# A new order table and new transfer times in the planner of a cluster-attention and expert-attention kernel

## The chip, the cores and the metric

The kernel runs on one core of one Trainium2 chip. The metric is the device time of one execution in microseconds (us), as the median of several runs of the same program. The kernel before has three runs, 741.66, 745.32 and 745.89 us, so its median is 745.32 us. One further execution was taken with the hardware profiler.

## What is computed

The reference is two attentions, one after the other (B = 4, S = 768, eight heads of 64, then four experts of 64 on 512 columns):

```python
q_assign = argmax(q_n @ c_n)          # 16 clusters a head; the same for the keys
scores = where(q_assign == k_assign, scale * q @ k.T, -1e9)
x = softmax(scores) @ v               # batch x sequence x 512
logits = x @ w_gate                   # top 2 of 4 experts, softmax over the two
for e in range(E):                    # causal attention of each expert
    ye = softmax(causal(scale * (x @ wq[e]) @ (x @ wk[e]).T)) @ (x @ wv[e]) @ wo[e]
    out += gate_e * ye
```

## The kernel before

The work is cut into 24 visits, numbered n: sixteen pairs of heads (n = 0 to 15) and eight pairs of experts (n = 16 to 23). For a pair of heads, `attention_operands` loads k, q and v, turns k and q on TensorE (L627), finds the clusters, and puts the operands for the scores into one of three sets of tiles, `tk` and `tq`, by DMA: the high and low parts of k and q, and the one-hot cluster rows (`place_rows`, four transfers for q and four for k). For a pair of experts `moe_operands` makes k and q from x (L871), and `moe_values` makes v and the gates: a chain of very small DVE instructions (L940 to L952), one exponential, five more small ones (L958 to L962), then a transpose on TensorE (L967).

`core(n)` is the same for both. Row products (L1085) give the scores of 128 queries against all keys; DVE takes their maximum (L1095); the maxima are turned (L1107) and go by DMA into `tq` as one more row, so that the second product, of scores laid out key block by key block (L1159, L1160), comes out with the maximum subtracted. ACT takes the exponential of each key block into a tile p (L1165), in the expert stage POOL clears what lies above the diagonal (L1170), and the products with v (L1203) sum p times v into `av`. They run as a **visit**: for most pairs of heads one visit takes all six key blocks of a half of the queries, 24 instructions of 128x384 in the profile. Sums over the p tiles (L480 on POOL or L481 on DVE, by the table) give the denominators, which go through a product with ones (L1223), a DMA to DRAM (`sd`), back (`r`), a reciprocal, to DRAM (`rd`) and back spread out (`rb`).

Nothing is left to a scheduler on the chip. Each piece of work is an `op` (L278) with an engine, a duration in the planner's eyes, what it comes after and which buffers it uses; some have a second engine that may take them (`alt`). `ORDER` (L37 to L216) is a table of the numbers of these ops, one list for each engine, which says in what order each engine runs them and, for ops with a choice, on which engine. `Plan.run` walks the table, gives buffers their slots by the times it works out, and emits the code. All DMAs are issued by SP, in the order of its list. The times that the planner assumes for a transfer are a pair (issue, move), such as `(0.45, 1.65)` for a load of q or k, plus `REACH` from the end of issue to the start of the move (L259). They do nothing on the chip by themselves: they decide which order a search finds and which slot a buffer gets. The waits on the chip come from what each instruction reads and writes. A transfer also waits for the landing of the one eight places ahead of it, since eight semaphores are shared in turn.

Two things in the planner matter below. An op that is marked `port` isn't placed beside work on POOL. And `needs` (L289) can give a dependence with a lead: the op may start before that piece is done. Before the change a visit of products with v waits, in the planner, for all its p tiles, and frees all of them at its end.

## Time and profile before

| | us |
|---|---|
| median of three runs | 745.32 |
| profiled execution, own time | 740.65 |
| its span, first to last instruction | 738.4 |
| PE busy / DVE busy / ACT busy / POOL busy | 707.2 / 552.6 / 369.5 / 335.0 |

The own time of the profiled execution is 2.25 us more than its span, and 4.67 us less than the median of the runs. PE is TensorE's matmuls, PEld its weight loads, DVE VectorE, ACT ScalarE, POOL GpSimd and SP the engine that issues the DMAs. A matmul of 384 columns counts as 0.34 us busy, but the next one starts 0.17 to 0.18 us later: they are pipelined, so a busy PE isn't PE at its peak, while an idle one is a real wait. An entry such as `[2.88 <-DMA tk<-xh]` in a list in order of time is the idle time ahead of the instruction and what ended it.

### The profile page before, as it was taken

The numbers are of one execution on the slowest core, as the hardware profiler recorded it, in microseconds if no ns is written. First come the engines' busy times: TensorE is split into PE (matmuls) and PEld (weight loads), VectorE is DVE, ScalarE is ACT, GpSimd is POOL, SyncE is SP. The second block draws the span as 40 slices with busy tenths as digits, with TensorE's granted clock in tenths as the row PEclk, the third lists the DMA queues.
The fourth block names the chain that finished last, engine by engine and source line by source line (L and its number), as shares of the span: only waits on it lengthen the run. The fifth ranks groups of instructions, "written<-read, shape, count | busy, mean of one in ns | idle before, by whom it ended". The sixth has DMA issues, their size and how long they took to land.

```text
span 738.4 us, 13669 instructions
## 1 busy us (share of the span) xinstructions
PE 707.2 (96%) x4607; PEld 531.0 (72%) x4607; DVE 552.6 (75%) x1249; ACT 369.5 (50%) x912; POOL 335.0 (45%) x267
## 2 busy tenths in 40 slices
PE   6889999999999999999999999989999999999997
PEld 5656757667676676676666689758877987987676
DVE  7978878878888788788778767783497389658733
ACT  4455647556565465466466542444353345434541
POOL 5034357664763864865786442153422223200530
PEclk9999999999999999999999999999999999999999
DMA  7796546485766686664776563525454545354223
GB/s 206 151 200 151 140 116 170 123 220 171 196 156 178 171 217 168 171 186 120 177 203 157 152 167 91 147 73 147 129 131 111 148 123 152 87 139 142 74 67 129
DMA packets 79793, 109.98 MB, mean 149 GB/s; under 512 B 23936, under 2 KB 63212, under 8 KB 79724
## 3 DMA queue, kind: packets, MB, share of 16 engines
q1 hardware_dynamic: 79724, 109.11, 56.8%
q8 instruction: 37, 0.61, 0.4%
q14 instruction: 32, 0.26, 0.1%
HBM read 36.54 MB, written 12.91 MB: 67 GB/s over the span
## 4 chain that ended last, share of the span: by engine, by line
PE 71%; DMA 10%; DVE 7%; SPq 6%; ACT 2%; issue 2%; POOL 1%; ACTq 0%; DVEq 0%; POOLq 0%
PE av L1203 15%; PE row L1085 11%; PE st L1159 9%; PE st L1160 9%; PE misc L871 9%; SPq L468 6%; PE misc L923 5%; PE misc L1312 4%; PE misc L627 3%; DMA tq<-hi 2%; PE misc L1223 2%; DVE mx L1095 2%; DMA qt<-in_q_dram 1%; DMA kt<-in_k_dram 1%; DMA tk<-hi 1%
## 5 line engine op out<-in xcount | busy, mean ns | idle before, releaser
L1095 DVE TENSOR_REDUCE mx<-row 128x1 f32<-128x384 f32 (+1 forms) x442 | 232.5, 548 | 60.5 <-PE row L1085 57.0
L1159 PE MATMUL st<-tq,tk 128*128 128x384 f32 (+2 forms) x528 | 182.4, 347 | 3.2 <-ACT p L1165 1.7
L1085 PE MATMUL row<-tk,tq 80*128 80x384 f32 (+3 forms) x506 | 172.5, 363 | 10.8 <-DVE mx L1095 3.9
L1165 ACT ACTIVATE p<-st 128x384 f32<-128x384 f32 (+2 forms) x304 | 128.3, 460 | 102.5 <-PE st L1160 63.0
L1160 PE MATMUL st<-tq,tk 97*128 97x384 f32 (+2 forms) x528 | 175.1, 333 | 0.1
L1085 PEld LDWEIGHTS row<-tk,tq 80*128 80x128 f32 (+1 forms) x506 | 93.2, 190 | 41.4 <-DVE mx L1095 16.9
L480 POOL TENSOR_TENSOR acc<-acc,p 128x768 f32<-128x768 f32 (+2 forms) x49 | 80.6, 1645 | 71.8 <-DVE acc L481 22.1
L1159 PEld LDWEIGHTS st<-tq,tk 128*128 128x128 f32 x528 | 100.3, 190 | 16.4 <-ACT p L1165 4.9
L1160 PEld LDWEIGHTS st<-tq,tk 97*128 97x128 f32 x528 | 100.9, 191 | 1.3 <-DMA tq<-mr 0.6
L1170 POOL TENSOR_SCALAR_AFFINE_SELECT p<-p 128x256 f32<-128x256 f32 x48 | 21.7, 465 | 116.5 <-ACT p L1165 103.9
L1165 ACT ACTIVATE xh<-st 128x384 f32<-128x384 f32 x112 | 50.8, 498 | 24.1 <-PE st L1160 23.7
L1165 ACT ACTIVATE xl<-st 128x384 f32<-128x384 f32 x112 | 51.0, 500 | 23.6 <-PE st L1160 23.2
L475 ACT ACTIVATE hi<-misc 128x384 fp32r<-128x384 f32 x74 | 36.7, 500 | 50.1 <-PE misc L871 28.9
L1203 PE MATMUL av<-p,vt 128*64 128x384 f32 x320 | 59.4, 495 | 0.0
L480 POOL TENSOR_TENSOR acc<-acc,xl 128x768 f32<-128x768 f32 x28 | 51.4, 1834 | 14.2 <-DVE acc L481 11.9
L480 POOL TENSOR_TENSOR acc<-p,p 128x768 f32<-128x768 f32 (+1 forms) x17 | 28.5, 1674 | 62.1 <-ACT p L1165 34.6
L480 POOL TENSOR_TENSOR acc<-acc,xh 128x768 f32<-128x768 f32 x28 | 51.2, 1831 | 8.8 <-DVE acc L481 4.8
L1274 POOL TENSOR_TENSOR xt<-avu,rb 128x384 f32<-128x384 f32 x32 | 32.3, 1016 | 49.2 <-DMA rb<-rd 36.9
L481 DVE TENSOR_TENSOR acc<-acc,p 128x768 f32<-128x768 f32 (+2 forms) x42 | 38.3, 913 | 13.4 <-POOL p L1170 10.5
L1093 DVE TENSOR_TENSOR row<-row,tri 128x128 f32<-128x128 f32 x96 | 28.1, 292 | 21.7 <-PE row L1085 21.6
L1203 PE MATMUL av<-p,vm 128*64 128x384 f32 (+2 forms) x288 | 41.5, 423 | 0.0
L1203 PE MATMUL av<-xl,vt 128*64 128x384 f32 x224 | 40.2, 491 | 0.0
(254 smaller groups left out, 1293.4 us busy)
## 6 DMA issues: line engine op xcount, KB each, us to landing
tq<-hi SPq DMA_DIRECT2D x91, 192.0 KB
tk<-hi SPq DMA_DIRECT2D x60, 192.0 KB
tk<-lo SPq DMA_DIRECT2D x46, 192.0 KB
tq<-lo SPq DMA_DIRECT2D x46, 192.0 KB
rb<-rd SPq DMA_DIRECT2D x46, 192.0 KB
vt<-in_v_dram SPq DMA_DIRECT2D x16, 384.0 KB
x<-xt SPq DMA_DIRECT2D x16, 384.0 KB
tk<-hi SPq DMA_DIRECT2D x16, 384.0 KB
```

Source lines behind the costliest of these rows:

```text
L468: SP.dma_start(*[x.bitcast(FT) if x.dtype == FR else x for x in (dst, src)])
L475: return op("act", t_act(n, sbuf), lambda: ACT.activation(dst(), src(), AF.Copy), due, after, use, alt=(MO["m_copy"], "dve", t_dve(n), lam ...
L480: ways = [("pool", t_pool(n), lambda: POOL.tensor_tensor(dst(), a(), b(), op=fn)), ("dve", t_dve(n), lambda: DVE.tensor_tensor(dst(), a(), ...
L481: ("dve", t_dve(n), lambda: DVE.tensor_tensor(dst(), a(), b(), op=fn))]
L871: PE.matmul(m()[:, :HW], w_[:, dc, es], x_[dc]()[:, c], start=(i == 0), stop=(i == 3 * DC - 1))
L923: PE.matmul(m()[:, :NV], x_[dc]()[:, ts], w_[:, dc, :], start=(i == 0), stop=(i == 3 * DC - 1))
L1085: PE.matmul(ps()[:, :w], Q[0:R, h, 0, c * 128:(c + 1) * 128], K[0:R, h, 0, i * w:(i + 1) * w], start=True, stop=True)
L1095: DVE.tensor_reduce(to, ps()[:, :w], axis=AX.X, op=OP.max)
L1159: PE.matmul(p()[:, o_:HW], K[:, h, 1, ks], Q[:, h, 1, qs], start=True, stop=False)
L1160: PE.matmul(p()[:, o_:HW], K[0:R, h, 0, ks], Q[0:R, h, 0, qs], start=False, stop=True)
L1165: ACT.activation(pt()[:, h, o_:HW], p()[:, o_:HW], AF.Exp, scale=SC)
L1203: PE.matmul(av()[h * 64:(h + 1) * 64, o_:HW], d["vv"](h, kc), pt()[:, h, o_:HW], start=(kc == 0), stop=(kc == nk - 1), tile_position=(0, 6 ...
```

## The change

Every list in `ORDER` is replaced. The numbers mean the same ops: the same 4015 ops are made, and only their order and, where they have a choice, their engine differ. PE's list keeps 1481 ops, 454 of them at the same place, and the others are moved by two places on average. SP's list keeps 452. DVE has 990 ops where it had 960, POOL 224 (246) and ACT 868 (876): 52 ops go from POOL to DVE and 30 from DVE to POOL. The lists in the source, and with them one line of it, are shorter, so line numbers of the changed kernel are one less than those here up to the products with v, and three more behind them. The rest of the diff is in the planner:

```diff
-    REACH, LANES = 1.8, 8
+    REACH, LANES = 2.05, 8
...
-            return t, op("sp", [(0.45, 1.65)], go, due, use=[t])
+            return t, op("sp", [(0.6, 1.6)], go, due, use=[t])
...
-            need_row = [op("sp", 4 * [(0.63, 0.29)], place_rows(Q, 0), c2 + 8, [o_r] + free, [rows]),
-                        op("sp", 4 * [(0.63, 0.29)], place_rows(K, 1), c2 + 8.2, [o_r] + free, [rows])]
+            need_row = [op("sp", 4 * [(0.64, 0.25)], place_rows(Q, 0), c2 + 8, [o_r] + free, [rows]),
+                        op("sp", 4 * [(0.64, 0.25)], place_rows(K, 1), c2 + 8.2, [o_r] + free, [rows])]
...
-        o = op("dve", 2.38, go, t0 - 20, ready, [lg, t, s])
+        o = op("dve", 2.38, go, t0 - 20, ready, [lg, t, s], port=True)
...
-        o = op("dve", 0.84, go, t0 - 16, [o], [t, s, wt])
+        o = op("dve", 0.84, go, t0 - 16, [o], [t, s, wt], port=True)
...
-                    av_prev = op("pe", sum(t_av(HW - x[1]) for x in waiting), go, due + DUE["av"],
-                                 [e for x in waiting for e in all_exps[x[0]]] + d["v_ready"] + [av_prev],
-                                 [av] + [x[2] for x in waiting] + d["v_use"], mode=64)
+
+                    long = [t_av(HW - x[1]) for x in waiting]
+                    av_prev = op("pe", sum(long), go, due + DUE["av"],
+                                 [(e, sum(long[:i])) for i, x in enumerate(waiting) for e in all_exps[x[0]]] +
+                                 d["v_ready"] + [av_prev], [av] + d["v_use"], mode=64)
+                    for i, x in enumerate(waiting):
+                        plan.needs(av_prev, (), [x[2]], sum(long[i + 1:]))
...
-            stored[b, pr] = op("sp", [(0.35, 0.55)], lambda: dma(xdr[b][pr], xt()), t1 + 22, norms, [xt])
+            stored[b, pr] = op("sp", [(0.6, 1.1)], lambda: dma(xdr[b][pr], xt()), t1 + 22, norms, [xt])
```

Other transfers get new pairs of the same kind, each by 0.02 to 0.25 us in its issue time. With the new `needs`, a visit may start, in the planner, when its first key block is ready, each later block being due only when the products ahead of it are done, and each p tile is free when its own products are.

Three places of the order follow. The first is SP in the start of the kernel, around the transfers for the second pair of heads (`tk_105`, `tq_106`; `rows` are the one-hot cluster rows, `vt` is a load of v, `qt` a load of q). Before:

```order
L468 DMA vt_396<-in_v_dram 128x2x384
L468 DMA tq_104<-lo_351 64x2x384 x2
L468 DMA tk_105<-xh_0_208 64x2x384 x2
L468 DMA vt_440<-in_v_dram 128x2x384
L468 DMA tk_105<-rows_458 16x384 x4
L468 DMA tk_105<-xh_0_218 64x2x384 x2
L468 DMA tq_106<-rows_458 16x384 x4
L468 DMA tq_106<-xl_0_484 64x2x384 x2
L468 DMA tk_105<-xh_0_208 64x2x384
```

After:

```order
L467 DMA tq_104<-hi_335 64x2x384 x2
L467 DMA tq_104<-lo_341 64x2x384 x2
L467 DMA tk_105<-xh_0_215 64x2x384 x2
L467 DMA tk_105<-xh_0_211 64x2x384
L467 DMA qt_455<-in_q_dram 128x2x384
L467 DMA tq_106<-rows_449 16x384 x4
L467 DMA tk_105<-rows_449 16x384 x4
L467 DMA tk_105<-xh_0_211 64x2x384 x2
L467 DMA tq_106<-xl_0_481 64x2x384 x2
```

The last transfer of k's high part, which stood behind everything else of the pair, now stands ahead of the cluster rows; the load of v for the third pair is gone from here (it comes much later), and the load of q for the third pair has come in, just ahead of the rows.

The second place is SP around the load of q for the tenth pair of heads (`qt_3183`, in the change `qt_2895`). Before:

```order
L468 DMA tq_108<-rows_3028 16x384 x4
L468 DMA tk_107<-rows_3028 16x384 x4
L468 DMA tq_108<-hi_3069 64x2x384 x4
L468 DMA tq_108<-lo_3081 64x2x384 x2
L468 DMA rd<-r_3017 128x12
L468 DMA tq_106<-mr_3153 1x3x128 x2
L468 DMA qt_3183<-in_q_dram 128x2x384
L468 DMA rb_3215<-rd 64x768 x2
```

After:

```order
L467 DMA rb_2857<-rd 64x768 x2
L467 DMA qt_2895<-in_q_dram 128x2x384
L467 DMA tk_107<-lo_2850 64x2x384 x2
L467 DMA sd<-ssb_2774 4x1x192 x2
L467 DMA x_114<-xt_2930 128x768
L467 DMA tk_107<-hi_2823 64x2x384
L467 DMA tq_106<-mr_2970 1x3x128 x2
L467 DMA kt_2986<-in_k_dram 128x2x384
L467 DMA tk_107<-hi_2823 64x2x384 x2
L467 DMA r_3021<-sd 128x12
L467 DMA tk_107<-rows_3027 16x384 x4
```

The load stood behind the transfers of the ninth pair's rows and q; now it stands ahead of all of them. The last row of the second list is the first of those transfers.

The third place is DVE around the gates of the first batch of the expert stage (`gs`, `gt`, `wt`). Before:

```order
L1093 TENSOR_TENSOR row_6429<-row_6429,tri 128x128
L1095 TENSOR_REDUCE MT<-row_6429 128x1
L1093 TENSOR_TENSOR row_6431<-row_6431,tri 128x128
L1095 TENSOR_REDUCE MT<-row_6431 128x1
L958 TENSOR_SCALAR gs_6311<-gs_6311 128x6
L959 RECIPROCAL gs_6311<-gs_6311 128x6
L960 TENSOR_TENSOR gt_6310<-gt_6310,gs_6311 128x24
L961 TENSOR_TENSOR gt_6310<-gt_6310 128x24
L962 TENSOR_TENSOR wt_6465<-gt_6310,gs_6311 128x6x4
L880 TENSOR_TENSOR lo_6355<-misc_6339,hi_6332 128x384
```

After:

```order
L957 TENSOR_SCALAR gs_6329<-gs_6329 128x6
L958 RECIPROCAL gs_6329<-gs_6329 128x6
L959 TENSOR_TENSOR gt_6328<-gt_6328,gs_6329 128x24
L960 TENSOR_TENSOR gt_6328<-gt_6328 128x24
L961 TENSOR_TENSOR wt_6405<-gt_6328,gs_6329 128x6x4
L879 TENSOR_TENSOR lo_6363<-misc_6349,hi_6345 128x384
L1099 TENSOR_REDUCE MT<-mx_6223 128x2x2
L480 TENSOR_TENSOR rows_6071<-vm_5779,s_5971 128x512
L480 TENSOR_TENSOR acc_6306<-acc_6306,p_0_6390 128x768
L480 TENSOR_TENSOR acc_6306<-acc_6306,p_0_6399 128x768
L1092 TENSOR_TENSOR row_6428<-row_6428,tri 128x128
L1094 TENSOR_REDUCE MT<-row_6428 128x1
```

The five gate instructions stood behind two row maxima of the next pair of experts; now they stand ahead of its first maximum, with a copy, a maximum and three sums between. On PE the transpose that reads `wt` (L967) stays near its place, five ops later in the list.

At three visits of products with v (the second halves of the fourth, seventh and tenth pair of heads) PE's list now has only one row product between the last scores whose exponentials the visit needs and its first product; before there were several products, of other pairs, between.

## The prediction

> **What bounds the kernel now.** First the page: the engines' shares, the slices, the chain that ended last.

> ```profile
> span 738.4 us, 13669 instructions
> PE 707.2 (96%) x4607; PEld 531.0 (72%) x4607; DVE 552.6 (75%) x1249; ACT 369.5 (50%) x912; POOL 335.0 (45%) x267
> PE   6889999999999999999999999989999999999997
> PE 71%; DMA 10%; DVE 7%; SPq 6%; ACT 2%; issue 2%; POOL 1%; ACTq 0%; DVEq 0%; POOLq 0%
> ```

> TensorE is busy in all slices but the first and the last few, and 71% of the chain is TensorE's own. A reordering takes no product away, so all it can win is waits of PE: 738.4 - 707.2 = 31.2 us of plain idle time, and what slow stretches cost. Next I read the list of waits of PE, and of its weight loads, which stand for the same sequencer.

> ```profile
> PE row L1085 <- DVE mx L1095: 3.9, 5, 1.2
> PE row L1085 <- DMA tq<-hi: 3.0, 5, 1.2
> PE row L1085 <- DMA tk<-xh: 2.9, 1, 2.9
> PE misc L627 <- DMA qt<-in_q_dram: 2.3, 3, 0.9
> PE misc L967 <- DVE wt L962: 1.7, 1, 1.7
> PE st L1159 <- ACT p L1165: 1.7, 2, 1.3
> PE misc L1107 <- DVE MT L1100: 1.5, 1, 1.5
> PEld row L1085 <- DVE mx L1095: 16.9, 30, 1.5
> ```

> The columns are total us, times, longest. No wait dominates: transfers 8.2 us in nine waits, and maxima on DVE 3.9 + 16.9 = 20.8 us in many short ones. Last I cut the stretches around three of these waits, for the granted clock.

> ```profile
> 40.00:43.50 3.50, 0.62 (x7) 0.28 (x3) 0.40 (x1) 2.09 (x7) 0.00 (x0) 1.00 0.93 230
> 481.00:485.80 4.80, 2.90 (x22) 1.53 (x19) 4.63 (x10) 2.33 (x6) 3.30 (x4) 1.00 0.24 52
> 485.80:489.20 3.40, 3.40 (x13) 2.60 (x14) 2.44 (x7) 0.63 (x2) 2.50 (x2) 0.50 0.22 85
> 489.20:492.60 3.40, 3.40 (x20) 1.97 (x22) 1.84 (x6) 2.24 (x5) 1.03 (x1) 1.00 0.00 0
> 557.50:560.90 3.40, 2.07 (x19) 1.24 (x16) 1.85 (x4) 2.10 (x5) 0.00 (x0) 1.00 0.33 64
> 560.90:564.30 3.40, 3.40 (x12) 3.30 (x12) 1.97 (x5) 0.83 (x3) 0.00 (x0) 0.50 0.01 3
> ```

> The columns are the stretch, its length, busy time and instructions of PE, PEld, DVE, ACT and POOL, then granted clock, DMA share and GB/s. Behind the waits of L967 (at 484.6) and L1159 (at 560.1) the clock is halved for 3.4 us; each such stretch loses 3.4 / 2 = 1.7 us of products.

> **The change part by part.** The new transfer times and the new leads do nothing on the chip; only the order does. The sum is made against the profiled execution's own time, 740.65 us.

> *Loads of q.* Three waits come from a load of q that SP issues late:

> ```profile
> 221.97 2.65 SPq L468 DMA_DIRECT2D tq<-rows  x4
> 227.25 2.64 SPq L468 DMA_DIRECT2D tq<-hi  x4
> 233.71 0.39 SPq L468 DMA_DIRECT2D qt<-in_q_dram  x1
> 237.21 0.52 PE L627 MATMUL misc<-identf,qt 128*128 128x128 f32 x3 [0.87 <-DMA qt<-in_q_dram]
> ```

> The load is issued at 233.71 and its reader stands ready at 236.3. In the new list it stands ahead of the pair's row and q transfers, so it is issued over 10 us earlier (the first of those transfers goes out at 221.97). The other two waits, of the 11th and 15th pair, have the same cause and cure. I take the whole row, 2.3 us; bounds 0 (SP held elsewhere) and 2.3.

> *Gates.* The five gate instructions of the first batch:

> ```profile
> 480.33 1.16 DVE L958 TENSOR_SCALAR gs<-gs 128x6 f32<-128x6 f32 x1
> 481.63 0.84 DVE L960 TENSOR_TENSOR gt<-gt,gs 128x24 f32<-128x24 f32 x1
> 482.50 1.73 DVE L961 TENSOR_TENSOR gt<-gt 128x24 f32<-128x24 f32 x1
> 481.42 1.02 POOL L1274 TENSOR_TENSOR xt<-avu,rb 128x384 f32<-128x384 f32 x1
> 482.38 1.81 POOL L480 TENSOR_TENSOR xl<-vt,xh 128x768 fp32r<-128x768 f32 x1
> L961 DVE TENSOR_TENSOR gt<-gt 128x24 f32<-128x24 f32 x4 | 2.3, 571 | 0.1
> ```

> L961 takes 1.73 us here, beside a busy POOL; the other three of its four executions take (2.3 - 1.73) / 3 = 0.19 us. So the chain is stretched by POOL's work and the transpose L967 waits for it. In the change the five stand two maxima earlier, and the planner keeps POOL away from them. I take away the wait, 1.7, and the half-clock stretch behind it, 1.7: 3.4 us together; bounds 0 and 3.4. The three sums that now follow on DVE are costed below.

> [...]

> *First row product of the second pair.* It waits 2.9 us (the row tk<-xh) for this part of SP's list:

> ```profile
> 27.11 0.72 SPq L468 DMA_DIRECT2D vt<-in_v_dram  x1
> 32.92 5.66 SPq L468 DMA_DIRECT2D tq<-rows  x4
> 38.68 1.33 SPq L468 DMA_DIRECT2D tq<-xl  x2
> 40.06 0.62 SPq L468 DMA_DIRECT2D tk<-xh  x1
> ```

> Four small transfers take 5.66 us at 32.92; four like them take 2.65 at 221.97 (above). SP was held by transfers eight places ahead that had not landed, the load of v among them. The change moves that load away and sends tk<-xh earlier, but puts a load of q just ahead of the eight row transfers, which can hold them in the same way. Bounds 0 and 2.9; I take half, 1.5.

> *The waits at 560 and 698.* L1159 waits 1.3 us for an exponential, with 1.7 us of half clock behind it, and L1107 waits 1.5 us for a maximum. The new order mixes other products in around both. Bounds 0 and 4.5; I take half, 2.2.

> *What stays.* The row products that wait for tq<-hi (3.0) end a run of ten transfers, eight of cluster rows and two of q, that stands unbroken in both lists, behind the same transposes on PE. I count nothing.

> *Visits of products with v.* Their number and length are the same; a visit is longer than what ACT needs behind it:

> ```profile
> 187.44 1.51 PE L1203 MATMUL av<-xh,vt 128*64 128x384 f32 x8
> 188.78 2.75 PE L1203 MATMUL av<-xl,vt 128*64 128x384 f32 x16
> 192.26 0.49 ACT L1165 ACTIVATE p<-st 128x384 f32<-128x384 f32 x1 [4.25 <-PE st L1160]
> ```

> From 187.44 to 191.5 PE does one visit of six key blocks and ACT has nothing for 4.25 us. Where the visit now begins one product behind its last scores, five blocks, 4.0 x 5 / 6 = 3.3 us, stand ahead of the products that need the last exponentials, two of 0.49 us. So they are hidden and I count 0. If ACT has other work queued there, each of three such visits can wait up to the longest wait for an exponential, 1.3: bound 3.9 lost. A gain I bound by the 1.7 us in which PE waits for p at all.

> *More work on DVE.* 52 pieces go from POOL to DVE and 30 back, 22 net, nearly all sums of p tiles:

> ```profile
> L480 POOL TENSOR_TENSOR acc<-acc,p 128x768 f32<-128x768 f32 (+2 forms) x49 | 80.6, 1645 | 71.8 <-DVE acc L481 22.1
> L481 DVE TENSOR_TENSOR acc<-acc,p 128x768 f32<-128x768 f32 (+2 forms) x42 | 38.3, 913 | 13.4 <-POOL p L1170 10.5
> 150.00:200.00 50.00, 49.36 (x328) 36.00 (x328) 43.40 (x95) 31.05 (x75) 32.66 (x21) 1.00 0.73 196
> ```

> 22 x 0.913 = 20.1 us more on DVE and 22 x 1.645 = 36.2 less on POOL. DVE goes from 552.6 to some 573 of 738 us; a sum lies hidden while PE has a row buffer free, but some will stand ahead of a maximum. Bounds 0 and 20.1. Scaling the 20.8 us of waits for maxima with DVE's busy time (573 / 553) adds 0.8; since the sums come in lumps of 0.913 I take twice that, 1.5.

> *New waits.* Most ops move by a place or two. I add 1.0, about one wait like those listed; bounds 0 and the 8.2 us that transfers cost today.

> The sum: 740.65 - 2.3 - 3.4 - 1.5 - 2.2 + 0 + 1.5 + 1.0 = 733.75. The median of the three runs lies 4.67 above the profiled execution, so the median of the changed kernel should be **738.4 us**, 6.9 or 0.9% below 745.32.

> **The rivals.**

> *All named waits go* and nothing comes back: 2.3 + 3.4 + 2.9 + 4.5 = 13.1, so 745.32 - 13.1 = 732.2 us. For it: the causes are late issues and one crowded DVE chain, which an order can cure. Against: the 35 short waits for DVE that no single place explains.

> *The table doesn't do what it says*: each wait cured opens another, and the time stays at 745 us (742 to 748). For it: PE's list hardly moves, and the run of transfers behind tq<-hi is the same. Against: the load of q has moved.

> *The half clock returns elsewhere.* If it doesn't hang on the gap ahead of it, as 2.9 us idle at full clock suggests, the two stretches stay: the gates give 1.7, and the places at 560 and 698 half of 2.8, so 733.75 + 1.7 + 0.8 + 4.67 = 740.9 us.

> *DVE becomes the bound.* Between 150 and 200 us it is busy 43.4 of 50 us already. If half of the 22 sums come ahead of a maximum for which both row buffers wait, and so hold PE for their length, PE loses 11 x 0.913 = 10.0 us. DVE is then too late for the other cures as well, and only the loads of q, which are SP's, are won: 745.32 - 2.3 + 10.0 = 753.0 us. From those 11 sums on it is slower by 1%. Against: DVE has idle time in every stretch, and the POOL sums that it takes over, 1.645 us each, held readers too.

> **How the numbers follow.** The forecast gets 0.44, all waits gone 0.19, nothing moved 0.17, the clock back 0.09, DVE the bound 0.11. About 1%, or 7.5 us, is what a measurement of this kernel can tell from no change, so faster means under 737.9. The forecast's own range, 733 to 743 (half of its gains more or less), is cut by that bound nearly in the middle: 0.24 to faster, 0.20 to the same. Faster is 0.24 + 0.19 = 0.43, the same 0.20 + 0.17 + 0.09 = 0.46, slower 0.11. The range that leaves a tenth out at each end goes from 728, beyond the first rival, to 752, short of the DVE rival.

> **What the changed profile would show.** No wait of L627 for qt<-in_q_dram. The gate instructions under 0.6 us each, L967 with no idle time ahead of it, and the clock at 1.00 there. The first row product of the second pair waiting 1 to 2 us. DVE busy 568 to 578 us and POOL 295 to 305. Waits for maxima at 21 to 24 us in all. No product with v waiting over 0.5 us for an exponential. I am wrong if PE's idle time does not fall by about 5 us from 31.2, if waits for maxima exceed 28 us, or if a wait for a load of q stays.

## The result, and the profile after

The changed kernel takes **723.24 us** (median of four runs, 721.82 to 724.66) against 745.61 us for the kernel before (four runs, 741.66 to 748.55). The ratio is 0.970, 95% interval 0.965 to 0.975: 3.0% faster, where 0.9% was forecast. A second series gave 723.02 us and 0.970 (0.967 to 0.973). Executions more than 1.5% above the fastest of the same kernel in a series, two of them of 1722 and 1724 us, are left out of the ratios and intervals. The profiled execution of the changed kernel takes 721.82 us, its span 720.1 us.

First its page: span, busy times, and the chain that ended last.

```profile
span 720.1 us, 13669 instructions
...
PE 702.6 (98%) x4609; PEld 529.2 (73%) x4609; DVE 567.5 (79%) x1279; ACT 365.8 (51%) x904; POOL 303.1 (42%) x245
...
PE 81%; DMA 7%; DVE 4%; SPq 3%; ACT 3%; issue 1%; ACTq 0%; DVEq 0%
```

The span falls by 18.3 us. PE's idle time falls from 31.2 to 17.5 (13.7 less), and PE's busy time by 4.6, of which 3.4 are the two half-clock stretches. Then the waits of PE:

```profile
PEld row L1084 <- DVE mx L1094: 9.7, 22, 0.6
...
PE misc L626 <- DMA kt<-in_k_dram: 5.9, 2, 4.4
PE st L1158 <- ACT p L1164: 1.8, 5, 0.6
...
PE row L1084 <- DMA tq<-hi: 1.3, 3, 0.5
...
PE misc L1106 <- DVE MT L1099: 1.0, 3, 0.6
...
PE misc L685 <- DVE oh L676: 0.8, 1, 0.8
...
PE row L626 <- DMA qt<-in_q_dram: 0.2, 1, 0.2
```

The waits for tk<-xh, for wt and the 3.9 us for maxima are gone. Behind the first 17 us the trace of before has 15 gaps of PE of half a microsecond or more, 17.6 us together; this one has 4, with 2.6 us. Where in the program that is, the busy time by stretch tells. Of the kernel before (columns as in the prediction's list of stretches):

```profile
20.00:120.00 100.00, 92.03 (x592) 64.56 (x592) 83.03 (x182) 54.55 (x134) 40.48 (x25) 1.00 0.68 155
...
420.00:520.00 100.00, 97.77 (x604) 78.15 (x605) 63.99 (x140) 44.05 (x114) 36.74 (x32) 0.98 0.50 134
520.00:620.00 100.00, 97.05 (x641) 80.32 (x640) 73.61 (x183) 42.38 (x115) 27.14 (x33) 0.98 0.51 135
```

And of the changed kernel:

```profile
20.00:120.00 100.00, 97.94 (x625) 68.17 (x623) 85.35 (x187) 56.90 (x139) 42.40 (x26) 1.00 0.68 163
...
420.00:520.00 100.00, 100.00 (x658) 83.09 (x657) 68.10 (x160) 43.79 (x117) 32.68 (x32) 1.00 0.50 135
520.00:620.00 100.00, 98.98 (x651) 81.27 (x650) 78.68 (x191) 45.98 (x119) 25.94 (x30) 1.00 0.47 123
```

The first 100 us win 5.9 us of PE's time, the passage to the experts (420 to 520) 2.2 and its clock, the next stretch 1.9 and its clock. Over the seven such stretches up to 700 us only one, 120 to 220, wins nothing (0.4 us less), so the gain is spread; DVE is busier in each of the three shown. The stretches are cut by time, and the changed kernel runs ahead, so a stretch holds somewhat later work there.

### The profile page after: what moved, and what is told of

It is laid out like the page before. It is cut to its first block, busy times and chain, and to the rows that moved or that the text cites. A ratio compares the mean times of both kernels' runs of the same rounds, so it can differ in the third digit from the quotient of the medians.

```text
span 720.1 us, 13669 instructions
## 1 busy us (share of the span) xinstructions
PE 702.6 (98%) x4609; PEld 529.2 (73%) x4609; DVE 567.5 (79%) x1279; ACT 365.8 (51%) x904; POOL 303.1 (42%) x245
## 4 chain that ended last, share of the span: by engine, by line
PE 81%; DMA 7%; DVE 4%; SPq 3%; ACT 3%; issue 1%; ACTq 0%; DVEq 0%
PE av L1202 20%; PE row L1084 11%; PE st L1158 11%; PE st L1159 10%; PE misc L870 9%; PE misc L922 5%; PE misc L1315 4%; SPq L467 3%; PE misc L1226 3%; PE misc L626 2%; DVE mx L1094 2%; DMA tq<-hi 2%; PE misc L650 1%; PE misc L1106 1%; DMA tk<-hi 1%
## 5 line engine op out<-in xcount | busy, mean ns | idle before, releaser
L1159 PE MATMUL st<-tq,tk 97*128 97x384 f32 (+2 forms) x528 | 174.0, 332 | 0.4 <-DMA tq<-mr 0.4
L1084 PE MATMUL row<-tk,tq 80*128 80x384 f32 (+3 forms) x506 | 170.0, 359 | 1.7 <-DMA tq<-hi 1.3
L1159 PEld LDWEIGHTS st<-tq,tk 97*128 97x128 f32 x528 | 100.4, 190 | 1.7 <-DMA tq<-mr 0.7
L479 POOL TENSOR_TENSOR acc<-acc,p 128x768 f32<-128x768 f32 (+2 forms) x39 | 64.8, 1660 | 74.5 <-DVE acc L480 38.0
L479 POOL TENSOR_TENSOR acc<-acc,xl 128x768 f32<-128x768 f32 x29 | 53.2, 1833 | 31.6 <-DVE acc L480 29.0
L1164 ACT ACTIVATE xh<-st 128x384 f32<-128x384 f32 x112 | 52.4, 499 | 19.5 <-PE st L1159 18.9
L479 POOL TENSOR_TENSOR acc<-p,p 128x768 f32<-128x768 f32 (+1 forms) x14 | 24.6, 1756 | 72.5 <-ACT p L1164 42.1
L479 POOL TENSOR_TENSOR acc<-acc,xh 128x768 f32<-128x768 f32 x24 | 44.0, 1831 | 22.0 <-DVE acc L480 19.4
L480 DVE TENSOR_TENSOR acc<-acc,p 128x768 f32<-128x768 f32 (+2 forms) x52 | 45.8, 880 | 5.4 <-POOL p L1169 1.7
L1277 POOL TENSOR_TENSOR xt<-avu,rb 128x384 f32<-128x384 f32 x28 | 28.2, 1021 | 35.3 <-DMA rb<-rd 31.3
```

The costliest lines, as they stand in the source:

```text
L479: ways = [("pool", t_pool(n), lambda: POOL.tensor_tensor(dst(), a(), b(), op=fn)), ("dve", t_dve(n), lambda: DVE.tensor_tensor(dst(), a(), ...
L480: ("dve", t_dve(n), lambda: DVE.tensor_tensor(dst(), a(), b(), op=fn))]
L1084: PE.matmul(ps()[:, :w], Q[0:R, h, 0, c * 128:(c + 1) * 128], K[0:R, h, 0, i * w:(i + 1) * w], start=True, stop=True)
L1159: PE.matmul(p()[:, o_:HW], K[0:R, h, 0, ks], Q[0:R, h, 0, qs], start=False, stop=True)
L1164: ACT.activation(pt()[:, h, o_:HW], p()[:, o_:HW], AF.Exp, scale=SC)
```

## Experiments

All times are medians; "before" is the kernel before on the same chip (743.75 to 745.73 us in the five series). In the edits, numbers are those of ops, in the lists of `ORDER`.

**The order, or the new numbers?** The new table under the old planner's code:

```diff
-    REACH, LANES = 2.05, 8
+    REACH, LANES = 1.8, 8
...
-                    for i, x in enumerate(waiting):
-                        plan.needs(av_prev, (), [x[2]], sum(long[i + 1:]))
```

> The new table run through the code of before (old transfer times, old dependences of the visits of products with v, no port marks). The order on every engine is the new one; only the planner's times, and with them the choice of a buffer's slot, can differ. Theory 'the order alone': 723 us, within 1% of the changed kernel. Rival 'the new numbers matter, through the buffer slots they choose': over 730 us.

Measured: 723.63 us, ratio 0.973 (0.969 to 0.978), the changed kernel's time within the scatter. The order does it; the new transfer times and leads do nothing on the chip that these runs could tell, as the prediction said. Whether the search needed the new times to find this order is not shown by any run.

**Where?** Two tables joined at a cut, on every engine (S holds the ops that start before the cut in the first table's plan):

```diff
+first, second = NEW, OLD        # new_then_old_420; the other way round in old_then_new_420
+ORDER[e] = [i for i in first[e] if i in S] + [i for i in second[e] if i not in S]
```

> The new table up to the work planned before 420 us (the first 13 to 14 pairs of heads), the old one behind it, on every engine. Theory 'spread': the first part keeps its 7 us (in the traces the changed kernel is 7.0 us ahead when the 14th pair ends): 738 us. Rival 'all in the passage to the experts': 744 us.

> The other half: the old table up to 420 us, the new one behind it. Theory 'spread': 18 - 7 = 11 us less, 733 us. Rival 'all in the passage to the experts': 726 us. If the halves don't add up to the whole, each needs the other.

Measured: 736.36 us (0.988, 0.983 to 0.994) and 731.95 us (0.983, 0.977 to 0.988), against 744.27: 7.9 and 12.3 us, together 20.2, nearly the whole. Each half keeps its own gain, as far as intervals of some 4 us either way can tell.

> The old table up to 420 us, the new one for what starts between 420 and 550 us, the old one again behind. In the traces 9 us of the gain arise between the 14th pair of heads and the third of experts. Theory 'spread, and additive': 745 - 9 = 736 us, the other 4 of old_then_new_420 being earned behind it. Theory 'the seams cost': two seams between tables open waits of 1 to 3 us, 738 to 742.

Measured: 737.65 us against 744.31 (0.993, 0.989 to 0.997): 6.7 of the 12.3 us of the second half arise between 420 and 550 us, though the two seams may cost some of it. The gain is spread, and additive by time within these intervals.

**Can the named waits be cured one by one in the old order?** Five maxima on DVE ahead of the pieces in front of them:

```diff
-531 273
+273 531
-702 445
+445 702
-703 570
+570 703
-1453 1337
+1337 1453
-3712 3715 3481
+3481 3712 3715
```

> Before, with five maxima on DVE moved ahead of the one or two pieces that stood in front of them (copies, splits, two sums), at the five places where a row product's wait for a maximum is idle time of PE, 3.9 us in all. Theory 'named waits': the 3.9 us go, 741.7 us against 745.6. Rival 'joint': the pieces pushed back are late next, and the time stays at 745.

Measured: 742.63 us against 743.75 (0.996, 0.993 to 1.000). The interval takes in both theories; against the cure speaks the profile, where PE still waits 3.1 us for maxima. Four cures together add to that the loads of q (1600, 1771 and 2455 at places 146, 171 and 245 of SP's list), the gates and the start:

```diff
-2978 2980 2845
+2845 2978 2980
...
-213 370 210 214 209 223 211 528
+213 211 210 214 209 223 370 528
```

> Before, with four cures at once and nothing else: three loads of q issued early on SP, the five gate instructions ahead of two maxima, the five maxima ahead of what stood in front of them, and in the start the load of v later and tk<-xh ahead of the cluster rows. Theory 'named waits': 2.3 + 3.4 + 3.9 + 2.9 = 12.5 us less, 733 us, that is most of the 18.3 us by which the spans differ. Rival 'joint': each cure opens another wait; 739 to 745 us, and the rest of the gain needs the whole table.

Measured: 742.75 us against 743.75 (0.998, 0.994 to 1.001). The span is 741.6 us with PE busy for 710.2: 31.4 us idle, as before. Two new waits show where the gain went. In the timeline of DVE and PE of all_named:

```profile
357.08 0.23 DVE L1250 RECIPROCAL r<-r 128x12 f32<-128x12 f32 x1 [3.12 <-DMA r<-sd]
357.22 0.95 DVE L1094 TENSOR_REDUCE mx<-row 128x1 f32<-128x384 f32 x2
...
357.77 0.45 PE L1084 MATMUL row<-tk,tq 80*128 80x384 f32 x1 [2.37 <-DVE mx L1094]
...
485.26 0.47 PE L1084 MATMUL row<-tk,tq 80*128 80x128 f32 x1 [4.69 <-DVE MT L1094]
```

The same reciprocal in the kernel before:

```profile
356.30 0.23 DVE L1251 RECIPROCAL r<-r 128x12 f32<-128x12 f32 x1 [0.86 <-DMA r<-sd]
```

DVE takes its list in order. It comes to the reciprocal earlier, the transfer lands no earlier, and the maximum behind the reciprocal holds PE for 2.4 us. At 485 the five gate instructions, now ahead of two maxima, are slow as before, and hold both maxima: PE waits 4.7 us there, where it had waited 1.7. So the gates were left in place in the next one and POOL's pieces beside them moved:

```diff
-2845 2971 2976 2984 2615 2982
+2845 2971 2976 2748 2984 2444 2615 2982 3110
```

> Before, with the gates of the first batch where they were, and the three pieces that POOL runs beside them (two sums of 1.83 and 1.81 us, one product of 1.02) given to DVE, behind the gates. Theory 'beside a busy POOL': the five gate instructions take 0.85 us instead of 4.1, their transpose waits for nothing and the half clock behind it goes: 3.4 us less, 742.2 against 745.6. Rival 'the pieces are late next': the 2.9 us of DVE work behind the gates holds maxima or sums, and the time stays at 745.

Measured: 743.98 us against 744.27 (1.000, 0.997 to 1.003). The wait for wt is gone, and some 7 us later PE waits 1.8 us for a copy of avu, which stands behind one of the moved pieces: the rival. Then one round of repairs of what all_named opened, without its gates (522 behind 785, 1927 behind 2188 and 3683 behind 3917 on DVE, 3415 and 3418 behind 3217 on ACT):

> The four cures of all_named followed through by one round of repairs: the gates stay at their place and the three pieces of POOL beside them go to DVE behind them; two reciprocals on DVE, which there held maxima while they waited 2.1 and 3.1 us for a transfer, stand behind the next maxima; a product that waited 1.2 us stands behind the last maxima of the last pair; two copies on ACT that waited for loads stand behind four exponentials. Theory 'named waits, followed through': 12.5 us of the first waits and 6.2 of the new ones are idle time of PE, and without gaps over 1.25 us in the experts the clock stays full there: 735 us or less. Theory 'joint': each repair moves the wait again, PE's idle time stays near 31 us and the time at 740 to 744.

Measured: 739.07 us against 744.31 (0.995, 0.992 to 0.998), 5.2 us less; PE's idle time in the profile is still 30.3 us. Neither theory's number; the idle time went as "joint" had it. In the old order a cured wait is mostly moved.

**The moved sums.** The 82 pieces that change between POOL and DVE, in the old order and taken back in the new one; each op stands in the other engine's list where its planned start falls. (Another 106 pieces, copies, change between ACT and DVE in the new table, 57 to DVE and 49 to ACT; no run moves those alone.)

```diff
-old table: dve 960 ops, pool 246 ops
+sums_over: dve 960 + 52 - 30 ops, pool 246 - 52 + 30 ops
-new table: dve 990 ops, pool 224 ops
+sums_back: dve 990 - 52 + 30 ops, pool 224 + 52 - 30 ops
```

> Before, with the 52 pieces given from POOL to DVE and the 30 others from DVE to POOL, each at the place where its planned start falls; nothing else of the new table. Giving the pieces back in the changed kernel cost 9.4 us (732.6 against 723.2). Theory 'the engines are worth that by themselves': 9 us less, 735. Theory 'only with the order made for them': DVE's list of before wasn't ordered for 22 more sums, so they stand ahead of maxima, and the time is 745 us or more; each sum ahead of an awaited maximum costs up to 0.9 us.

> The changed kernel, with the 52 pieces that it took from POOL to DVE given back to POOL and the 30 others back to DVE, each put in its new engine's list where its planned start falls. Theory 'the sums on DVE are neutral, the order of the maxima did it': within 1% of 723. Rival 'POOL's sums were what held PE': 735 us or more. By the prediction's own term (+1.5 for more work on DVE) it would be 1.5 us faster, 722.

Measured: sums_over 756.97 us against 744.27 (1.016, 1.012 to 1.020), sums_back 732.62 against 743.75 (0.986, 0.981 to 0.990). The same 82 moves cost 12.7 us in the old order, and undoing them in the new one costs 9.4. In both runs the moved pieces stand where no search put them, so a part of either cost can be their place and not their engine. Why they cost in the old order, the timeline of DVE, POOL and PE of sums_over shows:

```profile
157.31 2.38 DVE L479 TENSOR_TENSOR acc<-acc,xh 128x768 f32<-128x768 f32 x1
...
157.05 1.82 POOL L478 TENSOR_TENSOR acc<-acc,xh 128x768 f32<-128x768 f32 x1
...
160.21 0.44 PE L1083 MATMUL row<-tk,tq 80*128 80x384 f32 x1 [2.03 <-DVE mx L1093]
```

This sum on DVE, beside a sum on POOL, takes 2.38 us; such sums take 0.947 on average in the changed kernel (the next row). The maximum behind it comes late, and PE waits 2.0 us. Of all sums of 128x768 into acc on DVE in sums_over, the 45 that run beside no work of POOL take 0.94 to 1.01 us and the 14 beside it 0.95 to 2.58, 1.57 on average; the changed kernel has only four beside POOL, of 0.95 to 0.99.

```profile
L480 DVE TENSOR_TENSOR acc<-acc,xh 128x768 f32<-128x768 f32 x15 | 14.2, 947 | 0.1
```

> The changed kernel with only the 52 pieces given back from DVE to POOL, each where its planned start falls; the 30 others stay on POOL. sums_back (both) cost 9.4 us. Theory 'collisions and POOL's length': POOL gets some 85 us more work, sums wait in its list, p tiles and sums come late: 10 us or more slower, 733 or above. Theory 'the place on DVE is all': DVE is relieved, 723 or less.

> The changed kernel with only the 30 pieces given back from POOL to DVE, each where its planned start falls; the 52 stay on DVE. DVE gets 27 us more. Theory 'collisions on DVE' (a sum on DVE beside a sum on POOL takes 1.5 to 2.6 us instead of 0.95, and a maximum behind it is late): slower by the larger part of the 9.4 us, 729 or above. Theory 'DVE has room': 723 to 725.

Measured: 726.15 us (0.975, 0.968 to 0.982) and 727.15 us (0.977, 0.970 to 0.984): 3 and 4 us above the changed kernel, of 9.4 for both (between the means 2.6 us, interval -0.1 to 5.2, and 3.8 us, 1.1 to 6.5). POOL is busy for 386.0 us in the one, DVE for 588.8 in the other, and neither is the bound. In neither run did one of the two theories give the number; either group alone costs little, and it is not settled which collisions make the rest.

**Loads of q, late again in the new order.**

```diff
-sp places 146, 171, 245
+sp places 162, 182, 259        # q_late: behind rb<-rd; q_late_rb: directly ahead of it; q_late_mr: ahead of tq<-mr
```

> The changed kernel with the three loads of q (10th, 11th and 15th pair) back at the numbers in SP's list that they had before. Theory 'priced by its waits': the three waits of 0.5 to 1.0 us come back, 2.3 us, none long enough for the clock: 725.5 us. Theory 'joint': a late load delays the clusters' work behind it, 728 us or more. If the loads' place is worth nothing: 723.

Measured: 739.67 us against 744.31 (0.992, 0.990 to 0.995): the three loads at this place cost 16 of the 21 us. That is not their share in the gain: in the kernel before PE waited 2.3 us for them. In its timeline of SP and PE:

```profile
226.88 1.16 SPq L467 DMA_DIRECT2D rb<-rd  x2
228.12 0.54 SPq L467 DMA_DIRECT2D qt<-in_q_dram  x1
...
234.27 0.88 PE L626 MATMUL misc<-identf,qt 128*128 128x128 f32 x3 [3.78 <-DMA qt<-in_q_dram]
```

The load lies behind two broadcasts and is used 6.1 us after its issue; PE waits 3.8, 4.3 and 4.4 us (12.5 in all). In each wait 6.8 us of half clock begin:

```profile
232.10:238.90 6.80, 4.63 (x19) 4.02 (x23) 2.15 (x5) 1.50 (x4) 1.93 (x3) 0.50 0.91 213
266.30:273.10 6.80, 5.39 (x29) 3.78 (x29) 2.03 (x5) 1.75 (x4) 1.78 (x2) 0.50 0.27 62
378.90:385.70 6.80, 5.46 (x29) 3.78 (x29) 2.57 (x6) 0.98 (x2) 1.93 (x2) 0.50 0.84 212
```

PE is busy for 15.5 us of these, so 7.7 us of products are lost; PE's busy time has grown by as much, from 702.6 to 710.4. Waits and half clock make 20.2 us; 18.2 are left between the two profiled executions. The place in the list was the old one, but not the neighbour: before, the load stood ahead of the broadcasts.

> The changed kernel with the three loads of q directly ahead of the broadcasts rb<-rd, the neighbours that they had before; that is one place earlier in SP's list than in q_late, where they stood behind them and PE waited 3.8, 4.3 and 4.4 us. A broadcast pair takes SP 1.2 us, so the waits should be 2.6 to 3.2 us, 9 in all. Theory 'the clock goes with the gap' (gaps of 2 us and more were followed by half clock in 11 of 13 cases, gaps under 1.25 us in one of about 115): 9 + 3 x 1.7 to 3.4 = 14 to 19 us, less what buffers take up, 735 us. Theory 'only the waits count': 732 us or less.

> The same loads one transfer pair earlier still, ahead of the transfers of the maxima tq<-mr, which take SP 1.5 us: waits of 1.1 to 1.7 us, 4 in all, near the length at which the clock begins to go. Theory 'the clock goes with the gap': 727 us plus 1.7 for each gap that falls on it, 727 to 731, with more scatter than the changed kernel's 721.8 to 724.7. Theory 'only the waits count': 726 us.

Measured: 729.58 us (724.24 to 731.18; ratio 0.978, 0.971 to 0.986) and 726.06 us (723.11 to 729.98; 0.975, 0.966 to 0.984). In the profile of q_late_rb two waits of 0.75 and 1.01 us are left (1.8 in all, not 9), in that of q_late_mr none, and no half clock stands behind them. The waits were too small to decide between the theories on the clock; what the runs give is that one step in SP's list, past two broadcasts, is worth 10 us.

```profile
229.23 0.39 SPq L467 DMA_DIRECT2D qt<-in_q_dram  x1
229.71 1.16 SPq L467 DMA_DIRECT2D rb<-rd  x2
...
233.20 0.52 PE L626 MATMUL misc<-identf,qt 128*128 128x128 f32 x3 [0.75 <-DMA qt<-in_q_dram]
```

These rows of q_late_rb show it: ahead of the broadcasts the load is used 4.0 us after its issue, not 6.1. The other loads that PE waits for agree: 3.9 us in q_late_rb, 6.3 and 5.6 in q_late.

**Two more waits taken up in the new order.**

```diff
-36 356
+356 36
...
-879 718
+718 879
```

> The changed kernel with two of its last waits of PE taken up: the load of k of the third pair goes out ahead of a transfer of the first pair (PE waits 1.5 us for it), and a subtraction of 2.0 us on DVE stands behind the cluster work that waits for it (0.8 us). Theory 'named waits': 2.3 us less, 721 us. Theory 'joint': 723 us as before, the transfer passed over is late next.

> The changed kernel once more, next to the version with two more waits taken up. 723 us, its clock at 0.998 to 1.0 in each run and its runs within 4 us of one another, since it has no gap of PE over 1.25 us behind the first 16 us; before scatters over 15 us.

> The changed kernel with the load of k of the third pair ahead of a transfer of the first pair and the 2.0 us subtraction behind the cluster work. Theory 'named waits' as before: 2.3 us below the changed kernel, 721. Theory 'joint': the same as the changed kernel.

Measured: 722.17 us; then, side by side, 720.92 us (718.95 to 724.88) against 723.02 us (721.26 to 727.25) for the changed kernel, which scattered over 6 us, more than I had written; in its profile here a wait of 1.6 us for a load of v was followed by half clock. Over both series the means are 721.8 (12 runs) and 723.5 (10 runs): 1.7 us less, interval 0.1 to 3.4, where the waits were 2.3; side by side alone the means differ by 2.3, interval -0.5 to 5.0. So in the new order two named waits, cured, seem worth about their length, by a margin just clear of noise.

## Why the prediction was wrong

The direction was right, and the named waits went as forecast; the sum was nearly three times too small. In the profiled executions' own times, forecast -6.9, measured -18.8 us. The rows say where the time went, not that each could be won alone: of the same cures in the old order (all_named) 1 us was left.

| term | forecast | measured | from |
|---|---|---|---|
| loads of q | -2.3 | -1.7 | all idle time ahead of the transposes of q (L627/L626) behind the start, 2.3 to 0.6 |
| gates | -3.4 | -3.4 | wait for wt 1.7 to 0, clock 1.00 |
| first row product of the second pair | -1.5 | -2.9 | no wait for tk<-xh |
| waits at 560 and 698 | -2.2 | -2.9 | idle ahead of L1159 3.2 to 2.5, of L1107 1.5 to 1.0; clock 1.7 |
| what stays | 0 | -1.7 | tq<-hi 3.0 to 1.3 |
| visits of products with v | 0 | 0 | no product with v waits for an exponential |
| more work on DVE | +1.5 | -3.9 | waits of PE for maxima 3.9 to 0 |
| a wait that the sum left out | | -1.8 | first row product of the first pair, for cluster work |
| new waits | +1.0 | +1.5 | kt 4.8 to 5.9, oh 0.4 to 0.8 |

These make -16.8. Of the other 2.0 us, 1.2 are busy time of PE beyond the half clock, 0.5 lie between span and own time, and the rest is in gaps under half a microsecond. The wait left out has its row in the list of waits of the kernel before:

```profile
PE st L1085 <- DVE misc L670: 1.8, 1, 1.8
```

**More work on DVE** is the step that failed: +1.5 forecast, -3.9 measured, 5.4 of the 11.9 us by which the sum missed. It took the waits for maxima to grow with DVE's busy time. DVE's busy time did grow, to 567.5 us (half a microsecond under the range given; it left out the 57 copies that come from ACT and the 49 that go there), and the waits of PE and of its weight loads fell from 20.8 to 9.7. In the rows of sums_over what sets them is which piece stands ahead of a maximum and whether POOL runs beside that piece: with the same 82 pieces moved, sums_over has 13.0 us of such waits on PE alone (the row below), the changed kernel none.

```profile
PE row L1083 <- DVE mx L1093: 13.0, 17, 2.0
```

A share of busy time can't price that. Nor were the 20.8 us a price: the rows of PE alone make up nearly all of the 27.3 us that PE idles up to its last product, so the 16.9 us of the weight loads are no further idle time of PE, and only the 3.9 could be won. The range's far end was right for the wrong order: the rival in which sums hold maxima gave 753.0, and sums_over measured 757.0.

**The first rival's floor** was too small, which is why 723 lay outside the range. "All named waits" was 13.1 us, since I summed only what I could explain: it left out 3.9 for maxima, 3.0 for tq<-hi and 1.8 in the start. All 15 gaps of half a microsecond or more make 17.6 us; with the two half-clock stretches that is 21.0, and the measured gain in own time is 18.8. A new search of the whole table is not a set of cures: it can reach each gap, and it lays all five lists anew. That the cures in the old order bring next to nothing (1 us of 12.5, 5 after a round of repairs) is measured; that only laying all lists anew together brings the other 16 us is what the halves and the failed cures leave, and no single run shows it. Which of the moved places carry it stays open.

**The offset** of 4.67 us between the profiled execution and the median was carried over as a constant. It isn't one: the changed kernel's is 1.4. Over 69 runs of the kernel before (736.9 to 750.6 us) the mean granted clock goes from 0.981 to 1.000, and the time is 739.1 + 6.3 us for each percent that the clock lacks (correlation 0.79); the mean clock is 0.992. In ten runs of the changed kernel it is 0.999. So some 0.7 x 6.3 = 4.4 of the 20.6 us between the mean times are half clock, and the profiled execution of the kernel before was a lucky one: 10 of the 69 runs were shorter. So 3.3 us of the miss in the median are the offset.

Right were: no wait of over 0.2 us for a load of q, the gates (the first is the row below; the other four take 0.14 to 0.20 us), L967 without idle time, POOL at 303.1, no loss in the visits of products with v, and that the numbers themselves do nothing. The load of q just ahead of the eight row transfers of the second pair did not hold them: they took 2.61 and 2.48 us.

```profile
467.92 0.17 DVE L957 TENSOR_SCALAR gs<-gs 128x6 f32<-128x6 f32 x1
```

The gates' cure needed POOL's list too: moved ahead of two maxima, but still beside POOL's sums, they took 4.7 us (all_named). In rows of the same instruction away from POOL's work and beside it a sum takes 0.947 (mean of 15) and 2.38 us, the fourth gate 0.18 and 1.73, the first gate 0.17 and 1.16 or, in all_named, 1.79. Being beside POOL is not enough: the four sums of 0.95 to 0.99 us in the changed kernel were beside it too. Why some are slowed no run here shows.

## What to carry to other kernels

Where every list of an in-order program is searched anew, take the sum of all gaps of the bounding engine and the half clock that they bring, averaged over runs, as what can be won; the waits that you can explain are only a part. A single cure in a tightly laid order can just move the wait, to the next transfer or to the next piece in the list (1 us of 12.5 was left here in the old order, 1.7 of 2.3 in the new one); price it low unless you can say what stands behind it. And price a piece moved to another engine by what stands behind it there and what runs beside it, not by the engine's share: the same 82 moves cost 12.7 us in the old order, and undoing them cost 9.4 in the new one.

## What the runs showed of the hardware

```profile
38.67:42.08 3.41, 1.91 (x16) 0.44 (x12) 1.48 (x3) 2.01 (x7) 0.10 (x1) 1.00 0.62 155
42.08:45.50 3.42, 2.04 (x13) 2.04 (x14) 1.49 (x4) 0.85 (x3) 0.00 (x0) 1.00 1.01 262
...
482.40:485.82 3.42, 1.52 (x14) 0.75 (x14) 3.28 (x8) 1.39 (x4) 1.92 (x3) 1.00 0.18 32
485.82:489.23 3.41, 3.41 (x13) 2.61 (x14) 2.45 (x7) 0.61 (x2) 2.51 (x2) 0.50 0.22 84
```

And gates_quiet, with the same gap in the start, of 2.8 us:

```profile
41.12:44.54 3.42, 0.66 (x4) 0.45 (x4) 0.10 (x1) 2.06 (x7) 0.00 (x0) 1.00 0.96 239
44.54:47.95 3.41, 3.41 (x14) 3.33 (x13) 2.62 (x5) 0.63 (x2) 0.00 (x0) 0.50 1.09 254
```

In the kernel before the gap of 2.9 us fell across two steps, 1.5 us idle in the one and 1.4 in the other, and the clock stayed; in gates_quiet it fell into one, with 2.8 idle, and the next step ran at half clock. Counted over the 3,932 such steps at full clock of the 20 profiles (20 to 700 us), a half-clock step followed in 21 of 24 with 1.5 us or more idle, in 5 of 17 with 1.2 to 1.5, and in 2 of 3,891 with less; in the trace of the kernel before alone in 1 of 2, 1 of 3 and none of 191. So the gap in the start cost nothing in the one run and 1.7 us of products, half of 3.41, in the other. That gaps of 1.2 to 3 us are such a draw, which falls anew in each run, is my reading of these counts. It fits the scatter of the kernel before, which goes with the mean clock (correlation 0.79, above); the changed kernel, which behind the first 16 us has no such gap in one of its two profiles and one in the other, scatters less (6 us over ten runs, against 14 over 69).

**A load behind broadcasts** rb<-rd was used 6.1 us after its issue, one ahead of them 4.0 us after (q_late and q_late_rb, rows above).
